# A Fourier-mixing block with a gated feed-forward: four instead of three passes of the sequence DFT as seven block products

## The chip, the cores and the metric

One core of a Trainium2 chip runs the whole kernel in one launch. The metric is device microseconds from launch to end. TensorE (PE in the profile) multiplies, VectorE (DVE) and ScalarE (ACT) prepare operands and drain results, GpSimd (POOL) helps in the later stages, and SyncE (SP) issues every DMA, in order, from one queue.

## The reference, cut to what matters

With S = 2048 tokens, D = 448 channels and 1792 hidden units, all fp32:

```python
def _A_ref(x, dft_seq_re, dft_seq_im, dft_hid_re, dft_hid_im):
    a = jnp.einsum("bsd,ed->bse", x, dft_hid_re)
    b = jnp.einsum("bsd,ed->bse", x, dft_hid_im)
    return jnp.einsum("ts,bse->bte", dft_seq_re, a) - jnp.einsum("ts,bse->bte", dft_seq_im, b)

def _B_ref(x, w_gate, w_up, w_down):
    h = _gelu(x @ w_gate) * (x @ w_up)
    return h @ w_down

h = x + _A_ref(_layernorm(x), ...)
out = h + _B_ref(_layernorm(h), ...)
```

## The kernel before, in words

**Precision.** Every fp32 operand is cut into an fp16 part `hi` and an fp16 rest `lo`. ScalarE writes the `hi` (`hi_part`, L108), VectorE the `lo` (`lo_part`, L112 or L114), and TensorE multiplies hi·hi, hi·lo and lo·hi (`TERMS`). "Halving" below means this cut.

**Stages.** First the DFT over the sequence, then over the channels, then gate and up, then down. The sequence DFT makes eight pairs `p` of 256 output rows, each with a real and an imaginary part. It runs in 64 steps (`N_STEPS`). Steps 0 to 15 make pairs 0 and 1; after that every pass of four steps makes one part of one pair. A plain step is 24 matmuls of 448 columns (`seq_mm`, L648) with one weight tile of 1024 columns, which needs one `hi` on ScalarE and one `lo` on VectorE. From step `FAST = N_STEPS - 12` = 52 a step is 42 matmuls of 224 columns (`fast_mm`, L520): the 2x2 block product is made of seven products instead of eight. Such a step needs four sums of weight blocks on VectorE (`fast_sums`, L471 to L474), the halving of the raw blocks (768 columns) and of the sums (1024 columns), and once for all passes the sums `t0` to `t7` of the blocks of x (`t_norm` on ScalarE, `t_sums`, `t_hi`, `t_lo`). After four such steps the seven sums are put together (`fast_out`: seven operations of VectorE, L548, in the order of the products) and halved.

**Between the steps** other work is laid by hand: a table `early` gives what stands ahead of a step's matmuls, a table `after` what follows its first or second half. There are four kinds:

- For every pair, at steps m and m+1, `hid_mm(p, 0)` and `hid_mm(p, 1)` multiply by the channel DFT: 21 matmuls each (L714), both into the one PSUM bank of `ps_tr`. `hid_add` (L724, on VectorE) adds the bank to the residual tile `hx`. m is 36 for pair 3, 44 for pair 4 and 52 for pair 5.
- Ahead of that, `z_turn` transposes the pair by four DMAs; behind it come the pair's layernorm sums (`ffn_stats`), and for pairs 0 to 3 its normalisation, its sums and its transposes (`ffn_norm`, `ffn_sums`, `ffn_split`, `ffn_transpose`).
- For ten of the fourteen blocks `f` of the gate and up weights (`DFT_F`): load, `sums`, two halvings in three steps, and a store to DRAM (`w_dram`). The blocks 0, 1 and 2 are halved last and also stay in SBUF, where the first three steps of gate and up read them.
- The loads and sums of `t0` to `t7`, with three input tiles `tx` for two that a load needs.

**Gate and up** (`GateUp`, L1027) takes one of the fourteen blocks at a time, in three banks X, Y, Z. The PSUM pool of the DFT is closed before, so these banks are those that the last passes used. Y is first filled by ScalarE from X and then added to by TensorE. For the first two blocks a small matmul (L1053) stands ahead, into columns of Y that no earlier matmul has written.

VectorE, ScalarE and SyncE each work their queues strictly in the order in which the program emits them.

Of the kernel before, what the change touches and what calls it, by code (L numbers as in the profile page):

```python
# [13 lines left out]
P = 128  # L14
S, D, DF = 2048, 448, 1792
# [17 lines left out]
def kernel(  # L33
# [39 lines left out]
    nc = tc.nc  # L73
    V, A, G, PE = nc.vector, nc.scalar, nc.gpsimd, nc.tensor
# [30 lines left out]
    w_dram = [dram.tile([P, 28 * P], F16, name=f"w_dram{f}") for f in range(NF)]  # L105
# [41 lines left out]
    def normed(dst, src, mv, r, g):  # L147

        V.tensor_scalar(dst, src, mv[:, g, 0:1], r[:, g : g + 1], op0=ALU.subtract, op1=ALU.mult)
# [7 lines left out]
    HD = D // 2  # L157
# [13 lines left out]
    def w_tile(name):  # L171
        return ring.tile([P, 28 * P], F16, tag="w", bufs=3, name=name)


    hops, hops_raw = {}, {}
# [27 lines left out]
    def ffn_stats(q, j, h):  # L203
        for g in range(2):
            ffn_moments(q, j, h, g)
        ffn_rstd(q, j)
# [4 lines left out]
    def down_load(n):  # L211
        place = (fpool, "dn_w", 3) if n > 1 else (fops, "xn" if n % 2 else "tt", 1)
        wd32[n] = place[0].tile([P, 4, HD], F32, tag=place[1], bufs=place[2], name=f"wd32_{n}")
        nc.sync.dma_start(wd32[n].rearrange("p (k c) d -> p k (c d)", k=2), w_down[n])
# [10 lines left out]
    def ffn_norm(q, j, h):  # L225
        tag = f"h{q}_{j}"
        mv, r = moments.pop((q, j))
        xn = fops.tile([P, 2, D], F32, tag="xn", name=f"xn_{tag}")
        for g in range(2):
            normed(xn[:, g, :], h[:, g, :], mv, r, g)  # L230
        ffn[q, j] = xn

    def ffn_bias(q, j):
        mv, r = moments[q, j]
        V.scalar_tensor_tensor(mv[:, :, 1], mv[:, :, 0], -1.0, r, op0=ALU.mult, op1=ALU.mult)

    def ffn_norm_act(q, j, h):

        tag = f"h{q}_{j}"
        mv, r = moments.pop((q, j))  # L240
        nb = mv[:, :, 1]
        xn = fops.tile([P, 2, D], F32, tag="xn", name=f"xn_{tag}")
        for g in range(2):
            A.activation(xn[:, g, :], h[:, g, :], AF.Identity, scale=r[:, g : g + 1], bias=nb[:, g : g + 1])
        ffn[q, j] = xn

    def ffn_sums(q, j, parts=range(4)):

        if 0 in parts:
            t = fops.tile([P, 960], F32, tag="tt", name=f"tt_{q}_{j}")  # L250
            ffn[q, j] = ffn[q, j], t
        xn, t = ffn[q, j][:2]
        sub = V.tensor_sub
        if 0 in parts:
            sub(t[:, 0:256], xn[:, 1, 0:256], xn[:, 0, 0:256])
        if 1 in parts:
            sub(t[:, 256:448], xn[:, 1, 256:448], t[:, 0:192])
            V.tensor_scalar(t[:, 448:512], t[:, 192:256], -1.0, None, op0=ALU.mult)
        if 2 in parts:
            sub(t[:, 512:704], xn[:, 1, 256:448], xn[:, 1, 0:192])  # L260
            V.tensor_scalar(t[:, 704:768], xn[:, 1, 192:256], -1.0, None, op0=ALU.mult)
        if 3 in parts:

            sub(t[:, 768:960], xn[:, 0, 256:448], t[:, 256:448])
# [31 lines left out]
    def ffn_split(q, j):  # L296
        ffn_hi(q, j)
        ffn_lo(q, j)

    def ffn_transpose(q, j, parts):  # L300
        xs = ffn[q, j][2]
        ops = hops[q if q > 1 else 0]
        c = (2 * q + j if q < 2 else j) * P
        for n in parts:
            s0, s1 = ((0, 8), (8, 16), (16, 22), (22, 25))[n]
            nc.sync.dma_start_transpose(ops[:, s0:s1, c : c + P], xs[:, s0 * P : s1 * P])
# [110 lines left out]
    N_STEPS = NT + 8 * (NP - 2)  # L417
# [32 lines left out]

    FAST = N_STEPS - 12
    A_RAW = ("A12", "A11", "A22")
    FORMS = ("S1", "S2", "S3", "S4")
    T_OPS = ("T1", "T3", "T4", "T2")
# [22 lines left out]
    def fast_places(n):  # L479
        ring = dict(tag="ws", bufs=6)  # L480
        return (dict(tag="raw", bufs=2, pool=prep), ring) if n == FAST + 2 else (ring, ring)

# [92 lines left out]
    def t_norm(j):  # L575
        for k in range(2):
            x_affine(tx[j][k], tx[j][k], 2 * j + 1 - k)
# [87 lines left out]
    def z_turn(p):  # L665
        z[p] = hidp.tile([P, 2, 7, 2 * P], F16, tag="z", name=f"z{p}")
        for g in range(2):
            for l in range(2):
                nc.sync.dma_start_transpose(z[p][:, l, :, g * P : (g + 1) * P], zs[p][:, g, l, :])
# [29 lines left out]
    hp = {}  # L699
    xr = x.rearrange("(k g j p) d -> k j p g d", k=2, g=2, j=4)  # L700

    def h_tile(q, j):
        hp[q, j] = pair_tile(f"hx{q}_{j}")
        nc.sync.dma_start(hp[q, j], xr[q // 2, 2 * (q % 2) + j])
# [3 lines left out]
    def hid_mm(p, g):  # L708

        pool, tag = (ps_dn, "a3") if p == NP - 1 and g else (ps_tr, "tr")  # L710
        y = ys[p, g] = pool.tile([P, 512], F32, tag=tag, name=f"y_{p}_{g}")
        for k in range(7):
            for m, (lz, lw) in enumerate(((0, 0), (0, 1), (1, 0))):
                PE.matmul(  # L714
                    y[:, :D],
                    z[p][:, lz, k, g * P : (g + 1) * P],
                    wh[:, lw, k, :],
                    start=k == 0 and m == 0,
                    stop=k == 6 and m == 2,
                )  # L720

    def hid_add(p, g):
        h = hp[p // 2, p % 2][:, g, :]
        V.scalar_tensor_tensor(h, ys[p, g][:, :D], 1.0 / D_SC, h, op0=ALU.mult, op1=ALU.add)  # L724

    def h_store(q, j):
        nc.sync.dma_start(h_dram[2 * q + j], hp[q, j])


    gu = {}  # L730
    DFT_F = ((13, 17), (12, 20), (11, 25), (9, 29), (7, 33), (5, 37), (3, 41), (0, 45), (1, 48), (2, 50))
    JIT_F = range(4, 11, 2)

    early, after = {}, {}

    def at(where, n, *what):
        where.setdefault(n, []).extend(what)
# [4 lines left out]

    for f, n in DFT_F:
        at(after, (n - 4, 0), lambda f=f: gu.update({f: Weights(f)}))
# [3 lines left out]
        at(after, (n + 3, 0), lambda f=f: gu[f].store())  # L748


    turns = [(16, 0), (20, 1), (25, 1), (32, 0), (40, 0), (48, 0), (57, 0)]
    for p, (n, half) in enumerate(turns):
        b, j = divmod(p, 2)
        m = (19, 24, 29, 36, 44, 52, 60)[p]
        at(early, m - 1, lambda b=b, j=j: h_tile(b, j))
        for g in range(2):

            at(after, (m + g, int(p == 6 and g)), lambda p=p, g=g: hid_mm(p, g), lambda p=p, g=g: hid_add(p, g))
        at(after, (n, half), lambda p=p: z_turn(p))
        at(early, m + 2 if p < 5 else N_STEPS - 7 + p, lambda b=b, j=j: ffn_stats(b, j, hp[b, j]))  # L760
        at(after, (m + 2, 0), lambda b=b, j=j: h_store(b, j))
        if b < 2:

            m += 2 if p == 3 else 0
            at(early, m + 2, lambda b=b, j=j: ffn_norm(b, j, hp[b, j]))
            at(early, m + 3, lambda b=b, j=j: ffn_sums(b, j))
            at(early, m + 4, lambda b=b, j=j: ffn_split(b, j))
            for k in range(4):
                at(after, (m + 5 + k // 2, k % 2), lambda b=b, j=j, k=k: ffn_transpose(b, j, (k,)))
    at(early, N_STEPS - 2, lambda: h_tile(NB - 1, 1))  # L770
    at(early, N_STEPS - 1, gelu_table)
    at(after, (N_STEPS - 2, 0), lambda: down_load(0), lambda: down_load(1))
    for j, n in ((4, 28), (5, 31), (6, 39), (2, 43), (3, 45), (0, 47), (1, 49), (7, 53)):
        at(after, (n - 2, 1), lambda j=j: t_load(j))
        at(early, n, lambda j=j: t_norm(j), lambda j=j: t_sums(j))
        at(after, (n, 0), lambda j=j: t_hi(j))
        at(after, (n, 1), lambda j=j: t_lo(j))


    fast_at = [FAST + n for n in (-4, -2, -1)] + list(range(FAST + 1, N_STEPS - 2))  # L780

# [34 lines left out]
    for n in range(N_STEPS):  # L816
        if n == 0:
            for key in first:
                seq_acc(*key, last=key == first[-1])
        elif n >= FAST and n % 4 == 0:  # L820
            fast_begin(n)
# [3 lines left out]
        if n + 3 < NT:  # L825
            x_load(n + 3)
        if n + 3 < FAST:
            seq_load(n + 5)

        if 0 < n < FAST - 3:  # L830
            seq_hi(n + 3)
# [6 lines left out]
        if n == 0:  # L838
            seq_lo(2)
        if n + 3 < FAST:  # L840
            seq_lo(n + 3)
# [53 lines left out]
        else:  # L895
            p, part, qq = step_of(n)
# [24 lines left out]
    seq.close()  # L921
    fpool = ctx.enter_context(tc.tile_pool(name="fpool", bufs=1, side="right", reuse_waits="tile"))
    wd = {n: fpool.tile([P, 2, 7, HD], F16, name=f"wd{n}") for n in range(NF // 2)}
    gw = {f: gu[f].w for f in range(3)}

    class Drain:


# [98 lines left out]
    class GateUp:  # L1027
# [21 lines left out]
        def x1(self):  # L1049
            self.X, self.Y = self.bank(0), self.bank(1)  # L1050
            if self.t < 2:

                PE.matmul(self.Y[:, D:], gw[0][:, :P], hops[0][:, 0, D:], start=False, stop=True, skip_group_check=True)  # L1053
            self.mul(self.X, "A11", "B11", True)
            A.activation(self.Y, self.X, AF.Copy)  # L1055

# [222 lines left out]
    for t in range(NF):  # L1279
        w = gu.get(t + 2) if t + 2 in JIT_F else None  # L1280
        n = PREP_AT.get(t)
# [90 lines left out]
    for t in range(NF, N_GU):  # L1372
# [37 lines left out]
        if ends:  # L1410
            p = now[-1] // NC
# [21 lines left out]
        for p, t0 in ended.items():  # L1433
            if p < 5 and t - t0 in (1, 2):
                n = 4 * (t - t0)
# [104 lines left out]
```

## Time and profile before

| | |
|---|---|
| median of 3 runs | 713.81 us (713.41 to 713.83) |
| the profiled execution | 712.2 us, of which its instructions span 710.2 us |
| PE busy | 703.0 us, 99% of the span |
| PE weight loads busy | 480.1 us, 68% |
| DVE busy | 531.8 us, 75% |
| ACT busy | 353.2 us, 50% |
| POOL busy | 119.6 us, 17% |
| steps 16 to 63 of the sequence DFT | about 78 to 346 us |

Busy times are sums of instruction durations. Neighbouring operations of one engine overlap by some hundredths of a microsecond, so the distance between two starts is the better price. A wait in brackets in the timeline is idle time just before an operation, with what ended it.

### The profile page before, as it was taken

How to read it: one execution, taken by the hardware profiler on the slowest of the kernel's cores; microseconds unless marked ns; L12 is line 12 of the kernel's file. 1: busy time of each engine (PE TensorE's matmuls, PEld its weight loads, DVE VectorE, ACT ScalarE, POOL GpSimd, SP SyncE). 2: the span in 40 equal slices, each digit the busy share in tenths (PEclk: the TensorE clock that was granted, in tenths of full speed). 3: DMA queues.
4: the chain of work that ended last, by engine and by line, in shares of the span. 5: the costliest groups of instructions: out<-in, count | busy, mean ns of one | idle time of the engine just before them, and what ended most of it. 6: DMA issues, size and time to landing. Idle time of an engine off the chain costs nothing.

```text
span 710.2 us, 13038 instructions
## 1 busy us (share of the span) xinstructions
PE 703.0 (99%) x4952; PEld 480.1 (68%) x4952; DVE 531.8 (75%) x1136; ACT 353.2 (50%) x656; POOL 119.6 (17%) x128
## 2 busy tenths in 40 slices
PE   9999999999999999999999999999999999999998
PEld 5555555555555555797744444469999999989897
DVE  7988637486848779998647787567777866799785
ACT  5776523162526454543436566545555453555531
POOL 0000000000000000000223333311141522352624
PEclk9999999999999999999999999999999999999999
DMA  8788539999898969653755867797797986877512
GB/s 272 244 250 262 124 137 232 238 320 246 207 305 237 269 209 223 257 139 112 173 179 191 280 211 199 199 319 245 192 323 256 258 282 231 295 268 272 206 37 79
DMA packets 116031, 159.42 MB, mean 224 GB/s; under 512 B 61952, under 2 KB 80512, under 8 KB 115968
## 3 DMA queue, kind: packets, MB, share of 16 engines
q1 hardware_dynamic: 115968, 158.60, 73.3%
q8 instruction: 38, 0.62, 0.3%
q14 instruction: 25, 0.20, 0.1%
HBM read 110.33 MB, written 34.34 MB: 204 GB/s over the span
## 4 chain that ended last, share of the span: by engine, by line
PE 95%; DVE 3%; DMA 1%; issue 0%; POOL 0%; SPq 0%; DVEq 0%; POOLq 0%
PE acc L648 33%; PE acc_d L1212 14%; PE pY L1010 14%; PE y L714 9%; PE pZ L1010 9%; PE pX L1010 9%; PE acc_f L520 7%; DMA hid<-hid_dram 1%; DVE dn_s L1175 1%; PE pw L102 1%; DVE dn_s L1174 0%; DVE dn_s L1176 0%; DVE dn_w L112 0%; DVE hops L112 0%; DVE hr L1476 0%
## 5 line engine op out<-in xcount | busy, mean ns | idle before, releaser
L648 PE MATMUL acc<-xs,ws 128*128 128x448 f16 x1248 | 238.0, 352 | 0.0
L648 PEld LDWEIGHTS <-ws 128*128 128x128 f16 x1248 | 122.0, 98 | 114.0 <-DVE ws L114 0.2
L1010 PEld LDWEIGHTS <-gw 128*128 128x128 f16 x1365 | 133.4, 98 | 42.9
L1212 PE MATMUL acc_d<-wd,dn_w 128*128 128x224 f16 x1008 | 111.2, 259 | 2.4 <-DVE dn_w L112 2.4
L1212 PEld LDWEIGHTS <-dn_w 128*128 128x128 f16 x1008 | 96.7, 98 | 5.2 <-DVE dn_w L112 3.2
L1104 POOL TENSOR_TENSOR hs<-hs,c 128x256 f32<-128x256 f32 (+1 forms) x42 | 55.3, 1316 | 225.1 <-ACT c L1102 150.3
L1010 PE MATMUL pY<-hops,gw 128*128 128x256 f16 (+1 forms) x595 | 89.9, 294 | 0.0
L114 DVE SCALAR_TENSOR_TENSOR ws<-wr,ws 128x1024 f16<-128x1024 f32 (+2 forms) x66 | 75.1, 1141 | 8.6 <-ACT ws L108 8.3
L108 ACT ACTIVATE ws<-wr 128x1024 f16<-128x1024 f32 (+2 forms) x66 | 63.8, 981 | 21.5 <-DMA wr<-in_w_seq_dram 20.8
L220 POOL TENSOR_TENSOR wd_s<-wd 128x448 f32<-128x448 f32 x7 | 9.4, 1349 | 342.8 <-DVE r_h L142 342.0
L714 PE MATMUL y<-wh,z 128*128 128x448 f16 x336 | 66.2, 352 | 0.0
L1010 PE MATMUL pX<-hops,gw 128*128 128x256 f16 (+1 forms) x385 | 61.7, 294 | 0.0
L1010 PE MATMUL pZ<-hops,gw 128*128 128x256 f16 (+1 forms) x385 | 61.7, 294 | 0.0
L714 PEld LDWEIGHTS <-z 128*128 128x128 f16 x336 | 32.9, 98 | 30.1
L1020 DVE SCALAR_TENSOR_TENSOR c<-pZ,u 128x256 f32<-128x256 f32 (+1 forms) x42 | 21.4, 510 | 37.8 <-PE pZ L1010 22.3
L520 PEld LDWEIGHTS <-ws 128*128 128x128 f16 x504 | 48.3, 98 | 0.9
L1010 PEld LDWEIGHTS <-gu_w 128*128 128x128 f16 x273 | 26.6, 98 | 31.9 <-issue 0.2
L1055 ACT ACTIVATE pY<-pX 128x256 f32<-128x256 f32 (+1 forms) x42 | 18.4, 439 | 59.3 <-PE pX L1010 58.9
L1066 ACT ACTIVATE u<-pY 128x256 f32<-128x256 f32 (+1 forms) x42 | 19.1, 454 | 55.6 <-PE pY L1010 55.5
L972 POOL TENSOR_TENSOR hr<-hr,v 128x224 f32<-128x224 f32 x56 | 41.8, 772 | 14.7 <-ACT v L940 13.8
L108 ACT ACTIVATE dn_w<-dn_s 128x640 f16<-128x640 f32 x48 | 35.0, 729 | 18.0 <-DVE dn_s L1176 18.0
L112 DVE TENSOR_TENSOR dn_w<-dn_s,dn_w 128x640 f16<-128x640 f32 x48 | 41.6, 867 | 2.0 <-ACT dn_w L108 1.9
(138 smaller groups left out, 880.3 us busy)
## 6 DMA issues: line engine op xcount, KB each, us to landing
gw<-w_dram SPq DMA_DIRECT2D x35, 896.0 KB, 5.4
wr<-in_w_seq_dram SPq DMA_DIRECT2D x100, 256.0 KB, 4.5
hid_dram<-hs SPq DMA_DIRECT2D x27, 512.0 KB, 5.9
hid<-hid_dram SPq DMA_DIRECT2D x54, 256.0 KB, 5.6
w_dram<-gu_w SPq DMA_DIRECT2D x14, 896.0 KB, 5.7
gu_raw<-in_w_gu_dram SPq DMA_DIRECT2D x28, 384.0 KB, 5.9
wr<-in_w_seq_dram SPq DMA_DIRECT2D x14, 512.0 KB, 5.2
x<-in_x_dram SPq DMA_DIRECT2D x16, 224.0 KB, 2.8
```

The lines of the kernel that those rows point to most:

```text
L108: A.activation(dst, src, AF.Copy, scale=scale)
L112: V.tensor_sub(dst, src, hi)
L114: V.scalar_tensor_tensor(dst, src, scale, hi, op0=ALU.mult, op1=ALU.subtract)
L520: PE.matmul(fast_sum(n, k), fast_a(n, i, lw, a), fast_b(j, lx, b), start=j == 0 and m == 0 and k % 2 == 0, stop=j == NT // 2 - 1 and m == ...
L648: PE.matmul(acc[key][:, :D], w[:, lw, block * P : (block + 1) * P], xs[c][:, lx, :], start=c == 0 and m == 0, stop=c == NT - 1 and m == 2,)
L714: PE.matmul(y[:, :D], z[p][:, lz, k, g * P : (g + 1) * P], wh[:, lw, k, :], start=k == 0 and m == 0, stop=k == 6 and m == 2,)
L972: op(x, x, m)
L1010: PE.matmul(ps, w[:, wl, wa + ws, :], ops[:, m + ms, :], start=first and n == 0, stop=last and n == len(terms) - 1, skip_group_check=True,)
L1020: V.scalar_tensor_tensor(dst, ps, SC, other, op0=ALU.mult, op1=ALU.add)
L1066: A.activation(self.u2, self.Y, AF.Copy, scale=SC)
L1104: G.tensor_mul(c22, c22, self.cols(self.c12))
L1212: PE.matmul(ps, w[:, la, a, :], wd[n][:, lb, b, :], start=n == 0 and m == 0 and opens, stop=n == NC - 1 and m == 2, skip_group_check=True,)
```

## The change

`FAST` moves from step 52 to step 48, so that the real part of pair 6 is made of seven products too. The gate and up blocks are halved four to ten steps sooner. Blocks 0 to 2 are stored like the others and reloaded at steps 57 to 59 (`gw_first`). The `t` tiles are made two to five steps sooner, two of them in neighbouring steps. The normalisation of pairs 0 to 3 moves from VectorE (`ffn_norm`) to ScalarE (`ffn_norm_act`, with a small `ffn_bias` on VectorE), and pair 3 loses a delay of two steps. The small matmul into Y grows from 64 to 288 columns.

```diff
-    FAST = N_STEPS - 12
+    FAST = N_STEPS - 16
...
-    DFT_F = ((13, 17), (12, 20), (11, 25), (9, 29), (7, 33), (5, 37), (3, 41), (0, 45), (1, 48), (2, 50))
+    DFT_F = ((13, 13), (12, 15), (11, 18), (9, 21), (7, 24), (5, 28), (3, 32), (0, 36), (1, 39), (2, 42))
...
+    def gw_first(f):
+        gw[f] = w_tile(f"gw{f}")
+        nc.sync.dma_start(gw[f], w_dram[f])
...
+    for f in range(3):
+        at(after, (N_STEPS - 7 + f, 1), lambda f=f: gw_first(f))
...
         if b < 2:
-            m += 2 if p == 3 else 0
-            at(early, m + 2, lambda b=b, j=j: ffn_norm(b, j, hp[b, j]))
+            at(early, m + 2, lambda b=b, j=j: ffn_bias(b, j), lambda b=b, j=j: ffn_norm_act(b, j, hp[b, j]))
...
-    for j, n in ((4, 28), (5, 31), (6, 39), (2, 43), (3, 45), (0, 47), (1, 49), (7, 53)):
+    for j, n in ((4, 26), (5, 30), (6, 38), (2, 41), (3, 43), (0, 45), (1, 46), (7, 48)):
...
-    gw = {f: gu[f].w for f in range(3)}
...
-                PE.matmul(self.Y[:, D:], gw[0][:, :P], hops[0][:, 0, D:], start=False, stop=True, skip_group_check=True)
+                PE.matmul(self.Y[:, HD:], gw[0][:, :P], hops[0][:, 0, HD:], start=False, stop=True, skip_group_check=True)
```

The program's order shows where this lands. First ScalarE at steps 38 and 39, behind the root `sd_h1_1` of pair 3's layernorm; `ws` are DFT weights, `gu_w` gate and up weights, `xn_h` the normalised pair, `tx6` the input of `t6`. Before:

```order
L129 ACTIVATE sd_h1_1_2179<-mv_h1_1_2172,eps_t_85 128x2
L108 ACTIVATE ws42_2215<-wr42_2096 128x1024
L108 ACTIVATE gu_w5_2167<-gu_s5_2102 128x512 x2
L394 ACTIVATE tx6_0_2157<-tx6_0_2157,affine_170 128x448
L394 ACTIVATE tx6_1_2158<-tx6_1_2158,affine_170 128x448
L108 ACTIVATE zs4_2021<-acc4_10_2040 128x448
```

And in the changed kernel:

```order
L129 ACTIVATE sd_h1_1_2222<-mv_h1_1_2215,eps_t_85 128x2
L244 ACTIVATE xn_h1_1_2231<-hx1_1_2046,mv_h1_1_2215,r_h1_1_2224 128x448 x2
L394 ACTIVATE tx6_0_2143<-tx6_0_2143,affine_170 128x448
L394 ACTIVATE tx6_1_2144<-tx6_1_2144,affine_170 128x448
L108 ACTIVATE t6_2256<-tx6_0_2143 128x448
L108 ACTIVATE t6_2256<-tx6_1_2144 128x448
L108 ACTIVATE ws42_2276<-wr42_2147 128x1024
```

The two normalisations of the pair now stand between the root and `tx6`, and `tx6` follows in the same step.

Second VectorE ahead of the addition `hx2_0` of pair 4's first half (step 44); `zs5` is a drained accumulator. Before:

```order
L584 TENSOR_TENSOR tx2_1_2348<-tx2_1_2348 128x224
L114 SCALAR_TENSOR_TENSOR zs5_2427<-acc5_00_2261,zs5_2427 128x448
L114 SCALAR_TENSOR_TENSOR zs5_2427<-acc5_01_2262,zs5_2427 128x448
L112 TENSOR_TENSOR t2_2431<-tx2_0_2347,t2_2431 128x448
L112 TENSOR_TENSOR t2_2431<-tx2_1_2348,t2_2431 128x448
L114 SCALAR_TENSOR_TENSOR ws47_2460<-wr47_2351,ws47_2460 128x1024
L724 SCALAR_TENSOR_TENSOR hx2_0_2407<-y_4_0_2480,hx2_0_2407 128x448
```

And in the changed kernel:

```order
L112 TENSOR_TENSOR t3_2500<-tx3_0_2424,t3_2500 128x448
L112 TENSOR_TENSOR t3_2500<-tx3_1_2425,t3_2500 128x448
L114 SCALAR_TENSOR_TENSOR ws47_2528<-wr47_2428,ws47_2528 128x1024
L471 TENSOR_TENSOR sums48_2531<-wr48_2466 128x256
L472 TENSOR_TENSOR sums48_2531<-sums48_2531,wr48_2466 128x256
L473 TENSOR_TENSOR sums48_2531<-wr48_2466 128x256
L474 TENSOR_TENSOR sums48_2531<-wr48_2466,sums48_2531 128x256
L114 SCALAR_TENSOR_TENSOR ws48_0_2532<-wr48_2466,ws48_0_2532 128x768
L114 SCALAR_TENSOR_TENSOR ws48_1_2533<-sums48_2531,ws48_1_2533 128x1024
L114 SCALAR_TENSOR_TENSOR gu_w2_2472<-gu_s2_2434,gu_w2_2472 128x512 x2
L724 SCALAR_TENSOR_TENSOR hx2_0_2477<-y_4_0_2561,hx2_0_2477 128x448
```

The whole preparation of step 48 and the last halving of block 2 have come ahead of the addition, and `t3` stands where `t2` stood.

Third TensorE where gate and up begin, behind the last product of step 63; `acc_f60_3` is the bank of the seventh product of the last pass, `pY_0` the bank Y of the first block. Before:

```order
L520 LDWEIGHTS ws63_0_3514
L520 MATMUL acc_f60_3_3436<-t7_3032,ws63_0_3514 128x224
L1053 LDWEIGHTS gu_w0_2595
L1053 MATMUL pY_0_3779<-hops0_163,gu_w0_2595 128x64
L1010 LDWEIGHTS gu_w0_2595
```

And in the changed kernel, with the waits that the program states:

```order
L520 LDWEIGHTS ws63_0_3639
L520 MATMUL acc_f60_3_3561<-t7_2805,ws63_0_3639 128x224
L1058 LDWEIGHTS gw0_3424 [waits DMAHW2_49]
L1058 MATMUL pY_0_3904<-hops0_163,gw0_3424 128x288 [waits DVE_49]
L1015 LDWEIGHTS gw0_3424
```

The first matmul of gate and up has gained a wait for VectorE, and its weights one for a DMA. In the built program `pY_0` and `acc_f60_3` now are the same PSUM bank (bank 5); before, the last pass used the banks 1, 2, 3 and 7, and the first block of gate and up the banks 4, 5 and 6.

More of the change, by code (lines that the diff above doesn't have):

```diff
@@ L727, in h_store @@
         nc.sync.dma_start(h_dram[2 * q + j], hp[q, j])
-    gu = {}
-    DFT_F = ((13, 17), (12, 20), (11, 25), (9, 29), (7, 33), (5, 37), (3, 41), (0, 45), (1, 48), (2, 50))
+    gu, gw = {}, {}
+    DFT_F = ((13, 13), (12, 15), (11, 18), (9, 21), (7, 24), (5, 28), (3, 32), (0, 36), (1, 39), (2, 42))
     JIT_F = range(4, 11, 2)
     early, after = {}, {}
+    def gw_first(f):
+        gw[f] = w_tile(f"gw{f}")
+        nc.sync.dma_start(gw[f], w_dram[f])
     def at(where, n, *what):
```

## The prediction

> **What bounds the kernel now.** I read the page first, for the busy shares and the granted clock.
>
> ```profile
> PE 703.0 (99%) x4952; PEld 480.1 (68%) x4952; DVE 531.8 (75%) x1136; ACT 353.2 (50%) x656; POOL 119.6 (17%) x128
> PEclk9999999999999999999999999999999999999999
> ```
>
> PE is 99% busy at the full granted clock in every slice, so the time is the sum of PE's work, and there is almost no wait that an edit could take away. VectorE has a quarter of its time free, but whether that is free where a result is due must be seen stage by stage. The chain that ended last, in order of time, shows the sequence DFT as a string of PE groups with no gap:
>
> ```profile
> 243.75 4.54 PE acc L648 x24
> 248.29 3.97 PE y L714 x21
> ...
> 287.76 4.03 PE acc_f L520 x42
> 291.78 3.97 PE y L714 x21
> ```
>
> A plain step costs 4.54 us and a fast step 4.03 us. The second half of pair 4's channel DFT, `hid_mm(4, 1)`, starts at 248.29, that of pair 5 at 291.78. Third I read VectorE's timeline between the additions `hid_add` (L724), because VectorE works its queue in order and an addition sits behind all that was emitted before it.
>
> ```profile
> 208.04 0.62 DVE L724 SCALAR_TENSOR_TENSOR hx<-y,hx 128x448 f32<-128x448 f32 x1 [5.02 <-PE y L714]
> ...
> 219.96 0.62 DVE L114 SCALAR_TENSOR_TENSOR zs<-acc,zs 128x448 f16<-128x448 f32 x1 [1.65 <-ACT zs L108]
> ...
> 238.12 0.62 DVE L114 SCALAR_TENSOR_TENSOR zs<-acc,zs 128x448 f16<-128x448 f32 x1 [1.47 <-ACT zs L108]
> ...
> 243.79 0.62 DVE L724 SCALAR_TENSOR_TENSOR hx<-y,hx 128x448 f32<-128x448 f32 x1 [2.84 <-PE y L714]
> ...
> 252.30 0.62 DVE L724 SCALAR_TENSOR_TENSOR hx<-y,hx 128x448 f32<-128x448 f32 x1 [3.37 <-PE y L714]
> ```
>
> The brackets are the margins: VectorE reached pair 4's first addition at 243.79 - 2.84 = 240.95 and waited. Both halves of a pair go into one PSUM bank, so `hid_mm(4, 1)` may not start until that addition has read the bank. Before, the addition was over by 244.4, four microseconds early, and PE never felt it.
>
> **The change part by part.**
>
> *The fourth fast pass.* Four steps at 4.54 us become four at 4.03: 18.16 - 16.10 = 2.06 us off PE. That is the whole of the gain, since nothing else shortens PE's work.
>
> *The first addition of pair 4 (step 44).* I count what VectorE has to do between the second addition of pair 3 (at 208.04, where it waits for PE in both kernels) and the first of pair 4. Over that stretch the program's order gains the preparation of step 48 (four sums, two halvings), the sums and halving of one more `t` tile, the sums of one more gate and up block and one halving of such sums; it loses two normalisations (L149). The prices are distances between starts in these rows:
>
> ```profile
> 222.71 0.93 DVE L149 TENSOR_SCALAR xn_h<-hx,mv_h,r_h 128x448 f32<-128x448 f32 x2
> ...
> 281.63 0.56 DVE L329 TENSOR_TENSOR gu_s<-gu_raw 128x384 f32<-128x384 f32 x1
> ...
> 283.37 0.42 DVE L471 TENSOR_TENSOR sums<-wr 128x256 f32<-128x256 f32 x1
> ...
> 287.24 1.02 DVE L114 SCALAR_TENSOR_TENSOR gu_w<-gu_raw,gu_w 128x512 f16<-128x512 f32 x2
> 288.18 1.15 DVE L114 SCALAR_TENSOR_TENSOR zs<-acc,zs 128x448 f16<-128x448 f32 x2
> 289.24 1.28 DVE L114 SCALAR_TENSOR_TENSOR gu_w<-gu_s,gu_w 128x512 f16<-128x512 f32 x2
> 290.45 0.62 DVE L724 SCALAR_TENSOR_TENSOR hx<-y,hx 128x448 f32<-128x448 f32 x1
> ...
> 293.71 1.23 DVE L114 SCALAR_TENSOR_TENSOR ws<-sums,ws 128x1024 f16<-128x1024 f32 x1 [0.31 <-ACT ws L108]
> 294.85 0.39 DVE L581 TENSOR_TENSOR tx<-tx 128x224 f32<-128x224 f32 x1
> ...
> 296.50 0.62 DVE L724 SCALAR_TENSOR_TENSOR hx<-y,hx 128x448 f32<-128x448 f32 x1
> 297.03 1.15 DVE L112 TENSOR_TENSOR t<-tx,t 128x448 f16<-128x448 f32 x2
> 298.10 0.42 DVE L471 TENSOR_TENSOR sums<-wr 128x256 f32<-128x256 f32 x1
> ...
> 301.98 0.42 DVE L471 TENSOR_TENSOR sums<-wr 128x256 f32<-128x256 f32 x1
> ...
> 309.43 0.42 DVE L471 TENSOR_TENSOR sums<-wr 128x256 f32<-128x256 f32 x1
> ```
>
> A step's preparation is 301.98 - 298.10 = 3.88, the sums of a `t` tile 296.50 - 294.85 = 1.65 and its halving 1.07, a block's sums 283.37 - 281.63 = 1.74 and a halving 290.45 - 289.24 = 1.21. The stretch grows by 3.88 + 1.65 + 1.07 + 1.74 + 1.21 - 0.93 = 8.6 us. VectorE's arrival moves from 240.95 to 249.55. Two waits inside the stretch (1.65 and 1.47, for drains that follow PE's pace) vanish when VectorE comes later: 246.4. A new one comes in step 38, where `tx6` now stands behind both normalisations on ScalarE in the same step:
>
> ```profile
> L244 ACT ACTIVATE xn_h<-hx,mv_h,r_h 128x448 f32<-128x448 f32 x6 | 4.2, 752 | 1.0 <-DVE mv_h L235 1.0
> L394 ACT ACTIVATE tx<-tx,affine 128x448 f32<-128x448 f32 x16 | 11.3, 749 | 1.7 <-DMA tx<-in_x_dram 1.7
> ```
>
> From the root's last small operation VectorE has nothing before the sums of `t6`, so it waits for two normalisations and two `tx`, four operations of 0.75 = 3.0, less its own first sum of 0.39: 2.6 us, and arrives at 249.0. The addition takes 0.54 to its successor's start, so it ends at 249.6, against 248.29: PE waits 1.3. On top come waits of VectorE for ScalarE's part of a halving, which shares the busier queue; the row at 293.71 shows 0.31 for one, and with three to four more of these the wait is 2.4. This is the value I take, since the row of such a wait is at hand, with 0 and 4.1 as ends: nothing if the new waits don't come, and 4.1 if a load of `tx` is late by 1.7 as well, which is what ScalarE waited for one in the second row above. What is queued behind the addition is the preparation of step 49.
>
> *The first addition of pair 5 (step 52).* From 252.30, where VectorE waits for PE in both kernels, to 290.45. Over it the order gains three preparations of fast steps in place of plain ones and the combination of the pass 48 to 51; it loses three blocks' halvings, two blocks' sums, and one pair of accumulator halvings. A plain preparation, and the one wait in the stretch that a later VectorE doesn't meet, are in
>
> ```profile
> 264.23 0.63 DVE L114 SCALAR_TENSOR_TENSOR zs<-acc,zs 128x448 f16<-128x448 f32 x1 [0.76 <-ACT zs L108]
> ...
> 265.83 1.22 DVE L114 SCALAR_TENSOR_TENSOR ws<-wr,ws 128x1024 f16<-128x1024 f32 x1
> 266.97 0.42 DVE L471 TENSOR_TENSOR sums<-wr 128x256 f32<-128x256 f32 x1
> ```
>
> Three times 3.88 - 1.14 is 8.2. The combination is (309.43 - 301.98) - 3.88 = 3.6. Off go 3 x (0.94 + 1.21) = 6.45, 2 x 1.74 = 3.5, and 289.24 - 288.18 = 1.06. That leaves +0.8, and the wait of 0.76 takes it back: VectorE comes at 290.5 again, or 291.4 with a ScalarE wait of 0.31 for each new preparation. But PE wants to start `hid_mm(5, 1)` 2.06 us sooner, at 289.7. With 0.54 for the addition the wait is 1.3 to 2.3, and I take 1.5. Ends: 0.5, if the ScalarE waits and half of the rest are absorbed, and 3, with 0.7 more from a late transpose of pair 5.
>
> *Where gate and up begin.* Here nothing is hidden. Bank Y of the first block is now the bank of the last pass's seventh product, so its small matmul waits for the last of the seven combinations. VectorE's row for them and PE's for the small matmul:
>
> ```profile
> 337.95 0.62 DVE L724 SCALAR_TENSOR_TENSOR hx<-y,hx 128x448 f32<-128x448 f32 x1 [1.46 <-PE y L714]
> ...
> 344.77 2.63 DVE L548 SCALAR_TENSOR_TENSOR e<-acc_f,e 128x224 f32<-128x224 f32 x7
> 345.80 0.19 PE L1053 MATMUL pY<-hops,gu_w 128*128 128x64 f16 x1
> ```
>
> The combinations end at 344.77 + 2.63 = 347.40, and PE would start at 345.80: +1.6. VectorE sets out on this tail from pair 6's addition, for which it waits on PE, so the two move together. Ends: 1.0 (one more matmul modelled too early) and 1.8.
>
> *The small matmuls* grow from 64 to 288 columns. A plain step has 24 matmuls of 448 columns in 4.54 us, 0.42 ns a column, so 224 more columns cost 0.095, and two such matmuls +0.2. *Stores and reloads* of blocks 0 to 2 go through SP at steps 57 to 59, over 20 us ahead of their use, and a reload took 5.4 us to land:
>
> ```profile
> gw<-w_dram SPq DMA_DIRECT2D x35, 896.0 KB, 5.4
> ```
>
> Those 20 us hide it; uncovered, it would cost those 5.4. *ScalarE* takes eight normalisations of 0.75, 6 us of work on an engine busy half the time; costed above where it delays `tx6`, elsewhere nothing.
>
> The sum is -2.06 + 2.4 + 1.5 + 1.6 + 0.2 = +3.7 us. On the profiled 712.2 that is 715.9. The median of the runs is 1.6 above the profiled execution, so the forecast for it is 713.8 + 3.7 = 717.5.
>
> **The rivals.**
>
> *VectorE's slack swallows both additions.* The point that decides is whether the additions are over by 248.29 and 289.7. Without the wait at `tx6` and the ScalarE waits the first ends at 246.4 + 0.5 = 247; for the second VectorE would have to come 1.3 us sooner than I count. For it: VectorE waits 35.7 us in all for `y`, in eleven waits of up to 5.6, so its additions are mostly early.
>
> ```profile
> DVE hx L724 <- PE y L714: 35.7, 11, 5.6
> ```
>
> Against it: by the count above neither stretch has that idle time left. Then only the bank at the start of gate and up is left: -2.06 + 1.6 + 0.2 = -0.2, 713.6, no change. If just the first addition is in time, it is +1.3, 715.1.
>
> *The DMA queue decides.* SP works in order, and a pair's four transposes hold it:
>
> ```profile
> 268.25 9.65 SPq L669 DMA_TRANSPOSE z<-zs  x4
> ...
> 312.72 5.43 SPq L669 DMA_TRANSPOSE z<-zs  x4
> ```
>
> They take 5.4 to 9.7 us, and the loads of `wr47`, `wr48` and `tx3` stand behind the transposes of pairs 3 and 4. If VectorE is late with what they transpose, the loads are late too and one delay feeds the next; a difference such as 9.65 - 5.43 = 4.2 on top of my sum, less the part of the waits that it overlaps (about 1), gives 720.7.
>
> *The clock drops.* In the opening, 48 matmuls of 128 columns, 2.6 us at 0.42 ns a column, take 4.39, and the largest single wait of PE that the table of waits lists for VectorE is short:
>
> ```profile
> 1.37 4.39 PE pw L102 x48
> ...
> PE acc_d L1212 <- DVE dn_w L112: 2.4, 2, 1.7
> ```
>
> PE waited 1.7 us in one piece with the clock at 9 in every slice. A wait of 4.1 us, my upper end for step 44, is outside what the trace shows; if PE had then to start again as in the opening, it would lose 4.39 - 2.6 = 1.8, which with the longer wait is 3.7 + 1.7 + 1.8 = +7.2, 721.0. [...]
>
> *All covers hold and the reuse of the bank costs nothing*: -2.06 + 0.2 = -1.9, 711.9. The order shows the wait for VectorE, so this asks that the combinations end 1.6 us sooner, for which no row speaks.
>
> **How the numbers follow.** The measurement can tell about 0.2%, 1.4 us. Chances: the forecast 0.44, only the second addition late (715.1) 0.17, both in time (713.6) 0.14, the DMA queue (720.7) 0.14, the clock (721.0) 0.05, all covers hold (711.9) 0.06. Slower is 0.44 + 0.14 + 0.05 + half of 0.17 = 0.71, the same 0.14 + 0.09 = 0.23, faster 0.06. The range from 713.2 to 721.0 leaves out the last case, a third of the slot at 713.6 and half of those at 720.7 and 721.0.
>
> **What would show it.** In the chain after, PE should have three new pieces: a wait of some 2.4 us for VectorE ahead of the L714 group of step 45, one of 1.5 ahead of that of step 53, and one of 1.6 ahead of the first small matmul into `pY`. The fast steps 48 to 51 should take 4.03 us each. VectorE should wait 2.6 us for ScalarE ahead of the sums of `t6`, and not at all ahead of `hid_add` of pairs 4 and 5, first half. If PE shows no wait ahead of step 45, my count of that stretch is wrong; if the small matmul doesn't wait for `e`, the bank is not the one I read.

## The result and the profile after

The changed kernel took 724.5 us (median of 4 runs, 721.66 to 726.86), the kernel before 713.61 (4 runs, 712.71 to 713.83): a ratio of 1.0153, with a 95% interval of 1.0125 to 1.0181. The change costs 10.9 us where 3.7 were forecast. The profiled execution after took 723.23 us with a span of 721.5, against 712.2 and 710.2.

The chain that ended last, first of before, then of after, at the same places: the first channel DFT of pair 0, the second half of pair 3, of pair 4 and of pair 5, the fast steps behind it, and the first product of gate and up.

```profile
94.50 3.97 PE y L714 x21
...
204.03 3.97 PE y L714 x21
...
295.76 28.17 PE acc_f L520 x294
...
345.99 1.29 PE pX L1010 x6
```

```profile
100.95 3.97 PE y L714 x21
...
210.48 3.98 PE y L714 x21
...
257.68 5.83 PE y L714 x21
...
302.30 4.13 PE y L714 x21
306.44 28.18 PE acc_f L520 x294
...
358.43 1.29 PE pX L1015 x6
```

| stretch | before, us | after, us | lost by then | lost in it |
|---|---|---|---|---|
| to pair 0's channel DFT | 94.50 | 100.95 | 6.45 | +6.45 |
| to pair 3's second half | 204.03 | 210.48 | 6.45 | 0 |
| to the end of pair 5's second half | 295.76 | 306.44 | 10.68 | +4.23 |
| to gate and up's first product | 345.99 | 358.43 | 12.44 | +1.76 |
| to the end of the span | 710.2 | 721.5 | 11.3 | -1.14 |

More than half is lost before 101 us, in a part of the kernel of which the prediction says nothing. The table of waits after (us in total, times, longest) names four waits of PE that before did not have:

```profile
PE y L714 <- DVE hx L724: 4.3, 2, 2.9
PE acc L648 <- DVE zs L114: 2.5, 1, 2.5
PE acc L648 <- DVE xs L112: 1.7, 2, 1.5
PE pY L1058 <- DVE e L548: 1.5, 1, 1.5
```

The first and the last are the three waits that were forecast. The other two are early. The DMA queue's timeline shows why, first before, then after:

```profile
47.70 0.33 SPq L372 DMA_DIRECT2D x<-in_x_dram  x1
...
57.80 0.91 SPq L324 DMA_DIRECT2D gu_raw<-in_w_gu_dram  x2
```

```profile
44.79 0.61 SPq L688 DMA_DIRECT2D wh_raw<-in_w_hid_dram  x1
51.94 0.81 SPq L324 DMA_DIRECT2D gu_raw<-in_w_gu_dram  x2
52.80 0.43 SPq L372 DMA_DIRECT2D x<-in_x_dram  x1
```

Block 13's load now stands at step 9, block 12's at step 11. Both take a buffer that `wh_raw`, the raw channel DFT, still held: they share the two buffers of one tag. SP stood from 45.4 to 51.9 and issued nothing, until VectorE had halved `wh_raw` (the row at 51.30 below ends at 51.92), and the load of `x` behind it went out 5 us late. At block 12's load SP stood again, from 55.2 to 64.1, and the last load of `x` went out 9 us late. VectorE's and PE's timelines after:

```profile
51.30 0.62 DVE L114 SCALAR_TENSOR_TENSOR wh<-wh_raw,wh 128x448 f16<-128x448 f32 x1
...
56.93 0.63 DVE L122 BATCH_NORM_STATS2 st_x<-x 128x6 f32<-128x448 f32 x1 [4.30 <-DMA x<-in_x_dram]
```

```profile
71.72 9.05 PE L648 MATMUL acc<-xs,ws 128*128 128x448 f16 x47 [1.50 <-DVE xs L112]
83.22 17.73 PE L648 MATMUL acc<-xs,ws 128*128 128x448 f16 x84 [2.45 <-DVE zs L114]
```

VectorE waits 4.3 us for `x` (and 4.1 again at the last load), PE 1.5 for `xs`, and then 2.45 for the drains of pairs 0 and 1, which stand behind the late `x` and behind the blocks' sums. The second row holds something more: 84 matmuls of 0.19 us are 15.9, and they took 17.7. The windows of the trace, each 3.41 us long (busy time and count of each engine, then PEclk, the granted clock):

```profile
core 0: us, PE busy (x) PEld busy (x) DVE busy (x) ACT busy (x) POOL busy (x), PEclk, DMA share, GB/s
80.54:83.95 3.41, 0.96 (x6) 0.38 (x4) 3.34 (x8) 2.55 (x5) 0.00 (x0) 1.00 0.81 260
83.95:87.36 3.41, 3.41 (x11) 1.37 (x10) 3.41 (x7) 1.52 (x3) 0.00 (x0) 0.50 0.86 332
87.36:90.77 3.41, 3.41 (x20) 1.77 (x19) 3.41 (x6) 1.53 (x3) 0.00 (x0) 1.00 1.17 284
```

For one window behind the wait the clock is at a half, with 11 matmuls instead of 20. The same follows the wait ahead of pair 4's second half: its 21 matmuls take 5.83 us, against 4.13 behind the wait ahead of step 53, where the clock stays full. So one half clock costs 1.7 us here. A wait costs a little more than its bracket: the records of matmuls in a row overlap by 0.16 us (0.35 us each, at a distance of 0.19), and a wait takes this overlap away, which is why 21 matmuls behind one take 4.13 and not 3.97.

With this the loss can be added up. Up to gate and up's first product it is 12.44 us: waits of 1.7 + 2.45 + 2.93 + 1.35 + 1.5 = 9.9, 1.0 for the overlap at these six, 3.4 for two half clocks, less the 2.06 of the fourth pass, makes 12.2. The other 0.2 are the wider small matmul and the opening, where the clock first rose at 5.44 us instead of 4.63. Behind that 1.1 us came back, since PE's waits for `dn_w` add up to 0.7 us instead of 2.4. They range from 0.7 to 3.0 in the traces of this study, and nothing shows that this gain belongs to the change.

### The profile page after: what moved, and what is told of

Read it like the earlier page. It is cut to its first block, busy times and chain, and to the rows that moved or that the text cites. A ratio compares the mean times of both kernels' runs of the same rounds, so it can differ in the third digit from the quotient of the medians.

```text
span 721.5 us, 13233 instructions
## 1 busy us (share of the span) xinstructions
PE 705.7 (98%) x5024; PEld 488.2 (68%) x5024; DVE 539.3 (75%) x1159; ACT 362.5 (50%) x669; POOL 118.1 (16%) x128
## 4 chain that ended last, share of the span: by engine, by line
PE 71%; DVE 17%; DMA 5%; ACT 3%; issue 3%; SPq 1%; DVEq 0%; ACTq 0%
PE acc L648 14%; PE acc_d L1217 13%; PE pY L1015 13%; PE pZ L1015 8%; PE pX L1015 8%; PE y L714 8%; PE acc_f L520 6%; DVE ws L114 4%; DMA hid<-hid_dram 3%; DMA x<-in_x_dram 2%; ACT ws L108 1%; DVE xs L112 1%; DVE gu_w L114 1%; DVE st_x L122 1%; DMA wr<-in_w_seq_dram 1%
## 5 line engine op out<-in xcount | busy, mean ns | idle before, releaser
L648 PE MATMUL acc<-xs,ws 128*128 128x448 f16 x1152 | 221.9, 354 | 4.1 <-DVE zs L114 2.5
L648 PEld LDWEIGHTS <-ws 128*128 128x128 f16 x1152 | 113.1, 98 | 110.8 <-issue 6.9
L1015 PEld LDWEIGHTS <-gw 128*128 128x128 f16 x1482 | 144.8, 98 | 58.0 <-issue 1.7
L1015 PE MATMUL pY<-hops,gw 128*128 128x256 f16 (+1 forms) x646 | 101.9, 301 | 0.0
L714 PE MATMUL y<-wh,z 128*128 128x448 f16 x336 | 67.8, 359 | 4.3 <-DVE hx L724 4.3
L1015 PE MATMUL pZ<-hops,gw 128*128 128x256 f16 (+1 forms) x418 | 69.8, 301 | 0.0
L1015 PE MATMUL pX<-hops,gw 128*128 128x256 f16 (+1 forms) x418 | 69.8, 301 | 0.0
L520 PEld LDWEIGHTS <-ws 128*128 128x128 f16 x672 | 64.4, 98 | 0.9
L520 PE MATMUL acc_f<-t,ws 128*128 128x224 f16 x384 | 45.6, 259 | 0.0
L112 DVE TENSOR_TENSOR dn_w<-dn_s,dn_w 128x640 f16<-128x640 f32 x48 | 43.5, 907 | 2.0 <-ACT dn_w L108 1.9
```

The source lines that it names most:

```text
L112: V.tensor_sub(dst, src, hi)
L520: PE.matmul(fast_sum(n, k), fast_a(n, i, lw, a), fast_b(j, lx, b), start=j == 0 and m == 0 and k % 2 == 0, stop=j == NT // 2 - 1 and m == ...
L648: PE.matmul(acc[key][:, :D], w[:, lw, block * P : (block + 1) * P], xs[c][:, lx, :], start=c == 0 and m == 0, stop=c == NT - 1 and m == 2,)
L714: PE.matmul(y[:, :D], z[p][:, lz, k, g * P : (g + 1) * P], wh[:, lw, k, :], start=k == 0 and m == 0, stop=k == 6 and m == 2,)
L1015: PE.matmul(ps, w[:, wl, wa + ws, :], ops[:, m + ms, :], start=first and n == 0, stop=last and n == len(terms) - 1, skip_group_check=True,)
```

## The experiments

**The early loss: SP's queue.** The second and third `wh_raw` go to another ring; no engine's order changes. (`pair_tile` takes from the buffers of `hx`.)

```diff
-        t = wh_raw[n] = prep.tile([P, k1 - k0, D], F32, tag="raw", bufs=2, name=f"wh_raw{n}")
+        t = wh_raw[n] = pair_tile(f"wh_raw{n}") if n else prep.tile([P, k1 - k0, D], F32, tag="raw", bufs=2, name="wh_raw0")
```

> The changed kernel, with the second and third raw tile of the channel DFT (wh_raw) in buffers of the ring of hx, so that the first loads of gate and up blocks no longer wait for them; no instruction is moved on any engine. Theory (SP's queue): SP stood at the load of block 13, whose buffer VectorE freed only at 51.9, with the last loads of x behind it. Without that the x loads go out as before, PE's waits of 1.5 and 2.45 before 84 us and the half clock behind them (1.85) go, pair 0's channel DFT starts at 94.5 to 95.0 instead of 100.95, and the time falls by about 6 us, to 718.5. Rival (VectorE's work): it is the sums and halvings of blocks 13 and 12 ahead of the drains of pairs 0 and 1; then the wait of about 2.5 at the next pass stays with its clock, and only 1.7 us go: 722.8.

Measured: 718.99 us (4 runs, 717.18 to 719.63), 1.0079 of before (1.0059 to 1.0098). Its queue and its chain:

```profile
44.24 1.22 SPq L324 DMA_DIRECT2D gu_raw<-in_w_gu_dram  x2
47.37 0.33 SPq L372 DMA_DIRECT2D x<-in_x_dram  x1
```

```profile
94.65 3.97 PE y L714 x21
```

SP no longer stands, pair 0 begins at 94.65, and the median is 5.5 us below the changed kernel's. The rival is refuted: VectorE has the same work in the same order, and the drains are in time once `x` is.

The other way round, the kernel before with only these two blocks moved:

```diff
-    DFT_F = ((13, 17), (12, 20),
+    DFT_F = ((13, 13), (12, 15),
```

> The kernel before, with only the blocks 13 and 12 moved to steps 13 and 15 (loads four steps ahead of that). Theory (SP's queue): this alone brings the early loss, +6 to +6.5 us, about 720, with pair 0's channel DFT starting at 100 to 101 instead of 94.5 and no PE wait after that. Rival: the early loss needs the block that follows (11 at step 18) and the first stores too; then it is at most the 1.7 us of the late x, 715.3.

Measured: 717.58 us (716.68 to 718.45), 1.0064 of before (1.0045 to 1.0083). PE's timeline:

```profile
71.74 9.05 PE L648 MATMUL acc<-xs,ws 128*128 128x448 f16 x47 [1.30 <-DVE xs L112]
83.23 16.05 PE L648 MATMUL acc<-xs,ws 128*128 128x448 f16 x84 [2.44 <-DVE zs L114]
```

Both waits are back, 1.30 and 2.44, with two blocks alone. But the loss is 4.5 and not 6 to 6.5: the 84 matmuls took 16.05 us, so this wait of 2.44, as long as the 2.45 of the changed kernel, brought no half clock. That asked for an explanation of its own (below).

**The wait at step 45: VectorE's queue.** The preparation of step 48 is emitted in step 45.

```diff
-    fast_at = [FAST + n for n in (-4, -2, -1)] + list(range(FAST + 1, N_STEPS - 2))
+    fast_at = [FAST + n for n in (-3, -2, -1)] + list(range(FAST + 1, N_STEPS - 2))
```

> The changed kernel, with the preparation of fast step 48 emitted in step 45 instead of step 44, so behind the first addition of pair 4 instead of ahead of it. Theory (VectorE's queue): 3.9 us of VectorE's work leave the stretch, the wait of 2.93 ahead of the second half of pair 4 goes and with it the 1.86 that the half clock took behind it: -4.8 us, 719.7; the wait ahead of step 53 stays between 1 and 2. Rival (ScalarE or a load holds VectorE there, not the length of its queue): over 1.5 us of the wait stay, 722 or more.

Measured: 720.11 us (719.06 to 725.18). The waits of PE for the additions:

```profile
PE y L714 <- DVE hx L724: 1.6, 1, 1.6
```

One is left, that of step 53. So what stands ahead of the addition decides. This run moves two things at once, VectorE's work and its need of the weights of step 48, so by itself it does not tell them apart. The trace of the changed kernel does: VectorE shows no bracket for a DMA between 218 and 257 us, so there it was the work. The weights were close, though: in a1_wh_own the chain that ended last goes through their load, which lands at 245.75 us.

**The term of t6.** The trace after shows the wait ahead of the sums of `t6` and, without a bracket, the late addition:

```profile
222.43 0.39 DVE L581 TENSOR_TENSOR tx<-tx 128x224 f32<-128x224 f32 x1 [2.18 <-ACT tx L394]
223.08 0.39 DVE L582 TENSOR_TENSOR tx<-tx,tx 128x224 f32<-128x224 f32 x1 [0.26 <-ACT tx L394]
...
257.00 0.62 DVE L724 SCALAR_TENSOR_TENSOR hx<-y,hx 128x448 f32<-128x448 f32 x1
```

To see what those 2.44 us are worth, `t6` is made a step later, in step 39, where the kernel before makes it:

```diff
-    for j, n in ((4, 26), (5, 30), (6, 38), ...
+    for j, n in ((4, 26), (5, 30), (6, 39), ...
```

> The changed kernel with t6 made in step 39 instead of 38, so no longer in the step of pair 3's two normalisations. It weighs one term of the sum: VectorE's wait for ScalarE ahead of the sums of t6, which was put at 2.6 and is 2.44 in the trace of the changed kernel. Theory: the term is additive; VectorE no longer waits there, the 2.93 ahead of the second half of pair 4 fall to 0.3 to 0.8, and there is no half clock behind it. Rival: the loads set VectorE's arrival (tx3 and wr48 behind the transposes), and 1.5 or more of the wait stay. The early waits and the one at the start of gate and up stay in either case.

Measured: 726.69 us in one run. That is inside the 721.66 to 726.86 of the changed kernel, so the time alone tells nothing, and the trace is read instead. The wait of VectorE did not go but changed its name, and the queue did the rest (VectorE's timeline, then SP's, then PE's table of waits):

```profile
221.04 1.23 DVE L114 SCALAR_TENSOR_TENSOR ws<-wr,ws 128x1024 f16<-128x1024 f32 x1 [2.48 <-ACT ws L108]
...
253.75 0.42 DVE L471 TENSOR_TENSOR sums<-wr 128x256 f32<-128x256 f32 x1 [2.75 <-DMA wr<-in_w_seq_dram]
```

```profile
216.17 13.63 SPq L573 DMA_DIRECT2D tx<-in_x_dram  x2
```

```profile
PE y L714 <- DVE hx L724: 7.7, 2, 6.4
```

ScalarE's two normalisations delayed whatever VectorE did next, `t6` by 2.44 us in the changed kernel, the weights of step 42 by 2.48 here. And the next `tx` load needs one of three buffers that `t6` now gives back a step later: SP stands 13.6 us at it (7.4 in the changed kernel), the weights of step 48 land late, and PE waits 6.4. Of the 3.45 us that this is more than 2.93, the addition's being 1.8 us later is one half; the other is that PE came to this place 1.7 us sooner. The theory (an additive term) is refuted, and in this kernel the rival holds: the loads set VectorE's arrival. It is the early loss again, in another place: a load that waited 13.6 us for its buffer held everything behind it.

**The start of gate and up.** A first attempt hands the banks of the last pass to the products in another order:

```diff
+        if n == N_STEPS - 4:
+            fast_acc[n] = [fast_acc[n][k] for k in (3, 0, 2, 1)]
```

> The changed kernel, with the four PSUM banks of the last pass handed to the products in another order, so that the seventh product is in bank 7 and bank 5 (Y of gate and up's first block) holds the first two, which are drained first. Theory: PE's wait of 1.50 for the combinations ahead of the first matmul into pY goes, -1.5 us, 723.0 (the spread of the changed kernel is larger than that, so it is read from the profile: first pX matmul 0.3 us behind the last product instead of 1.8). Rival: the late VectorE is met again one block later, in bank 1 or 2 or at the transposes of pair 7, and less than 0.5 of it is gained by 400 us.

Measured: 723.6 us (721.51 to 724.62); the first matmul into `pY` waited 2.22. This says nothing of the theory: in the built program the pool has handed out banks 1, 7, 6 and 5 in the order of first use, as in the changed kernel, so the seventh product, begun last, got bank 5 again. What is needed is that it begins first. This goes into the next kernel, with the two repairs above:

```diff
-                one = [(i, k) for i in range(2) for k in ks] + [(i, 6) for i in range(2)]
+                one = [(i, k) for i in range(2) for k in ks]
+                sevenths = [(i, 6) for i in range(2)]
+                one = sevenths + one if n == N_STEPS - 4 else one + sevenths
```

(The small matmul of the first block then covers the last 64 columns again, since bank 5 now holds two products.)

> The changed kernel with three repairs at once: wh_raw in its own buffers (as a1_wh_own), the preparation of step 48 one step later (as a3_u48), and in the last pass the seventh product begun first, by which it gets bank 1 and bank 5 (Y of gate and up's first block) holds the first two products. Theory (three causes, independent): PE has no wait before step 45, none at step 45, 1.3 to 1.6 at step 53, at most 0.3 at the start of gate and up; no half clock; 713.1 - 2.06 + 1.5 + 0.1 + 0.1 = 712.8, equal to the kernel before. Rival (the causes are one: VectorE is late everywhere, and what is removed in one place comes back in the next): waits of over 2 us at step 53 or behind 345 us, 715 or more.

Measured: 712.77 us (11 runs, 711.51 to 714.66), 0.9993 of before (0.998 to 1.0005). PE's timeline at the start of gate and up and ahead of step 53 (this second row is cut by its window behind 7 of the 21 matmuls):

```profile
345.91 0.19 PE L1061 MATMUL pY<-hops,gw 128*128 128x64 f16 x1
```

```profile
291.74 1.49 PE L714 MATMUL y<-wh,z 128*128 128x448 f16 x7 [1.63 <-DVE hx L724]
```

The bank's wait is gone, the one of step 53 is there, and the forecast of 712.8 from independent causes holds; the rival's 715 or more does not come.

**The last wait.** To the repairs of c1_three is added that at step 52 the preparation of step 54 is emitted behind the addition instead of ahead of it. For that it becomes a function.

```diff
-        if n in fast_at:
+        def fast_prep(n):
             unit = fast_at.index(n) + FAST
...
+        if n in fast_at and n != 52:
+            fast_prep(n)
...
                     for what in after.get((n, m // 7), ()):
                         what()
+                    if n == 52 and m == 6:
+                        fast_prep(n)
```

> As c1_three, and at step 52 the preparation of step 54 is emitted behind the first half of the matmuls, so behind the first addition of pair 5 instead of ahead of it. Theory: VectorE reaches that addition 3.9 us sooner, the wait at step 53 goes as well, and the whole of the fourth pass is left: 713.1 - 2.06 + 0.2 = 711.3, faster than before by 1.8 us. Rival (the later preparation is missed by PE at step 54, or ScalarE's part of it): the wait moves to step 54 or 56 and 712.8 stays.

Measured: 710.94 us (8 runs, 710.27 to 712.24), 0.997 of before (0.9959 to 0.9981). The chain:

```profile
263.89 18.11 PE acc_f L520 x189
282.01 3.97 PE y L714 x21
285.98 4.02 PE acc_f L520 x42
290.00 3.97 PE y L714 x21
...
344.21 1.29 PE pX L1021 x6
```

No gap is left, 189 matmuls (4.5 steps) take 18.11, so 4.02 a step, and gate and up begin at 344.21, 1.78 sooner than before. This version beats both kernels, the one before by 2.0 us or 0.3%.

**The tables without the pass.** The changed kernel with three fast passes as before (and the small matmul back at 64 columns):

```diff
-    FAST = N_STEPS - 16
+    FAST = N_STEPS - 12
```

> The changed kernel with three fast passes, as before (FAST = 52, and the small matmul at 64 columns): what is left of the change are the earlier halvings, the reloads, the earlier t tiles and the normalisation on ScalarE. Theory: the early loss by SP's queue stays whole (3.7 to 6.4, with or without a half clock), and there is no wait at the additions and none at the start of gate and up: 717 to 719.5. Rival (the waits of pair 4 come from t6 behind the normalisations, not from the fourth pass): a wait of over 1 us at step 45 stays, 719 to 722.

Measured: 718.48 us (5 runs, 715.18 to 719.14), 1.0074 of before (1.0058 to 1.009). Its longest wait of PE before 350 us:

```profile
PE acc L648 <- DVE zs L114: 2.4, 1, 2.4
```

Beside it there is only one of 0.5 for the late `xs`, so the early loss is all that is left. The waits at the additions and at gate and up belong to the fourth pass on top of these tables, and the rival, by which `t6` alone brings the wait at step 45, is refuted.

**What halves the clock.** Two kernels that put waits of chosen length into the kernel before. The lines of d1_waits; d2_waits has 21, 21, 20 and 25 multiplications:

```diff
+        if g == 0:
+            for _ in range({0: 17, 1: 20, 3: 21, 4: 20}.get(p, 0)):
+                V.tensor_scalar(h, h, 1.0, None, op0=ALU.mult)
         V.scalar_tensor_tensor(h, ys[p, g][:, :D], 1.0 / D_SC, h, op0=ALU.mult, op1=ALU.add)
```

> The kernel before, with 17, 20, 21 and 20 multiplications of hx by 1 on VectorE ahead of the first additions of pairs 0, 1, 3 and 4, so that PE waits some 1.8, 2.3, 2.8 and 3.3 us ahead of the second halves (sizes rough). Theory from the traces so far (half clock for 3.41 us at a time, at steps of a 3.41 us grid): the clock halves in the window behind one in which PE was idle for more than a limit between 1.85 and 2.34 us, so a wait that the grid cuts in two brings none and an uncut one of 2.4 or more does. Rival 1 (a whole window must be idle): no half clock for any of them. Rival 2 (length alone): all waits over 2.4 bring one, whatever the grid.

> As d1_waits, with 21, 21, 20 and 25 multiplications, for waits of PE of about 2.4, 2.1, 1.9 and 4.0 us ahead of the second halves of pairs 0, 1, 3 and 4. Theory: half clock for 3.41 us behind a window of the grid in which PE was idle for over a limit that lies between 1.87 and 2.33; so none behind the wait of 1.9, one behind the wait of 4.0 unless the grid cuts it near its middle, and the other two by how the grid cuts them. Rival (a whole window must be idle): only the 4.0 could bring one, and only if it covers a window.

Measured, 721.1 and 725.47 us in one run each. The waits came out as 0.71, 1.64, 2.37 and 1.87 us, and as 2.43, 2.39, 1.62 and 4.03. In every trace that has a half clock before PE's last matmul, it comes in pieces of 3.41 us (once two of them), and their starts lie whole multiples of 3.41 us behind the first rise of the clock: a grid. In the changed kernel the first piece starts 78.51 us behind it, which is 23 of them, and the second 170.67 us, 50 of them, behind the end of the first. With it the idle time of PE in each window can be counted, for all PE waits over 1.8 us up to 360 us (behind that, no trace has a half clock ahead of PE's last matmul):

| kernel, wait at | length | idle in the windows it touches | half clock next |
|---|---|---|---|
| a1_wh_own, 248.4 | 3.10 | 1.71, 1.39 | no |
| b1_two_early, 80.8 | 2.44 | 0.90, 1.54 | no |
| c3_fast12, 79.7 | 2.44 | 1.35, 1.10 | no |
| a3_u48, 352.2 | 2.68 | 1.85, 0.83 | no |
| a4_ybank, 355.4 | 2.22 | 0.43, 1.79 | no |
| d1_waits, 255.2 | 1.87 | 1.87 | no |
| d2_waits, 102.8 | 2.43 | 0.53, 1.90 | no |
| d2_waits, 136.1 | 2.39 | 1.43, 0.95 | no |
| d2_waits, 255.0 | 4.03 | 1.93, 2.09 | no behind the first, yes behind the second |
| a5_t6, 69.6 | 2.17 | 2.17 | yes |
| a3_u48, 80.9 | 2.44 | 0.11, 2.33 | yes |
| d1_waits, 206.7 | 2.37 | 2.37 | yes |
| after, 80.8 | 2.45 | 2.45 | yes |
| a4_ybank, 69.8 | 2.57 | 2.57 | yes |
| a4_ybank, 253.7 | 2.76 | 2.76 | yes |
| after, 254.8 | 2.93 | 2.93 | yes |
| a5_t6, 253.1 | 6.38 | 0.41, 3.41, 2.56 | no, yes, yes |

The windows of d2_waits around its longest wait, columns as before:

```profile
253.54:256.96 3.42, 1.49 (x8) 0.69 (x7) 3.15 (x9) 0.00 (x0) 0.00 (x0) 1.00 1.12 320
256.96:260.37 3.41, 1.32 (x7) 0.68 (x7) 3.21 (x7) 0.00 (x0) 0.00 (x0) 1.00 0.45 163
260.37:263.78 3.41, 3.41 (x11) 1.37 (x10) 2.94 (x8) 0.75 (x2) 0.00 (x0) 0.50 0.01 2
```

This is the sharpest case: a window with 1.93 us of idle time brought nothing, one with 2.09 brought the half clock. Both ends come from this one trace. All seventeen cases agree with a limit between 1.93 and 2.09 us in one window. Both rivals are refuted: a whole window did not have to be idle (2.09 of 3.41 us were enough), and the length of the wait did not decide (3.10 us in a1_wh_own brought no half clock, 2.17 in a5_t6 did).

## Why the prediction was wrong

*The fourth pass.* Right: 4.02 us a step, and 1.8 to 2.0 us faster once nothing else is in the way (c2_four).

*The three waits.* Right in place and cause, and near in size: 2.93 for a forecast of 2.4 at step 45 (2.76 and 3.10 in two other traces), 1.35 for 1.5 at step 53, 1.50 for 1.6 at gate and up. Their sum is 5.8 for 5.5. c3_fast12 has none of them; c1_three takes two away and c2_four the third. The ledger behind the first was not additive as written: a5_t6 shows that the 2.6 us for `t6` (2.44 in the trace) are a wait for the normalisations that the next operation inherits. Of the two waits that the ledger took as gone, one is still there in the changed kernel with 0.60 us, about the 0.5 by which the first forecast was short. "The DMA queue decides", a rival with 0.14, was close there, as the chain of a1_wh_own shows, but did not decide in the changed kernel. (The five terms of the sum make 3.64, which the prediction writes as 3.7.)

*What failed* is the step that isn't there. The prediction costs the earlier halvings only in VectorE's two stretches, 208 to 290 us, and sets SP's part of the change at nothing but the stores and reloads of blocks 0 to 2. It names no load that moved, and so puts the early part of the kernel at no cost without a reason. The ten blocks move by four to nine steps, and blocks 13 and 12 carry theirs from steps 13 and 16 to 9 and 11, ahead of the last loads of `x` and into buffers that `wh_raw` held. SP stands there, these loads of `x` go out up to 9 us late, and PE waits before 101 us. That costs 4.5 us (b1_two_early, without a half clock) to 6.5 (the profiled execution after, with one). The two facts needed, the tag `raw` with two buffers and the place of the loads among those of `x`, stand in the code.

*The clock* was the second miss. It was a rival with a chance of 0.05, tied to a wait of 4.1. The case shows it behind waits of 2.45 and 2.93, at 1.7 us each: 3.4 of the 11.3 us in the profiled execution. The forecast counts no half clock behind its own three waits of 1.5 to 2.4. That was the author's estimate, and the trace of before could not show it: its longest wait within the matmuls was 1.7, less than the 1.93 that brought none in d2_waits.

With both, the sum is 3.7 + 4.1 (early waits) + 3.4 (clock) = 11.2, and the two profiled executions lie 11.0 apart. That this comes so close is luck: the 1.0 for the overlap lost at each wait and the 1.1 that the later stages happened to save nearly cancel.

## What to carry to other kernels

When a load is moved forward, list what stands behind it in its queue and who holds the buffer it asks for; here a load that waited 6.5 us for a buffer held up everything behind it, though the DMA engines had time to spare (41% busy from 45.4 to 51.9 us, while SP stood, against 70% before). When a preparation moves ahead of an addition that frees a PSUM bank, emit it behind that addition if it is not needed for some steps: the early load's own buffers brought 724.5 down to 719.0 us here, and two such moves and a bank brought that down to 710.9. Add to a PE wait of over 2 us the price of a half clock that may follow it, 1.7 us here.

## What the runs showed of the hardware

In the traces with a half clock ahead of PE's last matmul, the granted clock fell to a half for 3.41 us at a time, at whole multiples of 3.41 us behind its first rise (23 of them for the first piece in the changed kernel). Among the waits of the table it did so behind each window in which PE was idle for 2.09 us or more, and behind none with 1.93 or less. Each such window cost 1.7 us (17.73 against 16.05 for 84 matmuls, 5.83 against 4.13 for 21). The grid lay differently in the traces (first rise of the clock at 4.25 to 6.60 us), and a wait of the same length cost 1.7 us in one execution and nothing in another: 2.45 us in the changed kernel, all in one window, did, and 2.44 in b1_two_early, with 0.90 and 1.54 in two windows, did not. The four runs of the changed kernel show mean clocks of 0.998, 0.995, 0.995 and 0.993, at 721.66, 723.23, 726.86 and 725.77 us. By estimate that is one, two, two and three such windows, since each takes half of 3.41 us out of some 721, or 0.0024 of the mean. The clock is thus part of their spread, but not all of it: the second and the third differ by 3.6 us at the same clock. What the rest is stays open.

The wait at the start of gate and up varied from 1.5 to 2.7 us. VectorE's small operations at that place took 0.58 to 1.13 us where they ran beside GpSimd, and 0.15 to 0.17 where they did not. In a3_u48, with a wait of 2.68, VectorE's and GpSimd's timelines show:

```profile
350.65 1.06 DVE L143 TENSOR_TENSOR r_h<-r_h 128x2 f32<-128x2 f32 x1
```

```profile
350.55 1.13 POOL L222 TENSOR_TENSOR wd_s<-wd 128x448 f32<-128x448 f32 x1
```

Operations on two elements a partition that took 0.16 us elsewhere took about as long as the GpSimd operation that ran beside them. No run took GpSimd's part away, so that the one causes the other is a reading of the trace and not shown by an experiment.
